# An mLSTM cell followed by a Fourier mixing block and an MLP: four shape-changing products and five steps moved within the order of issue

## The chip, the cores and the metric

The kernel runs on one core of a Trainium2 chip. A core has engines that run side by side, each with its own queue of instructions: TensorE (PE, matrix products; PEld are its weight loads), VectorE (DVE), ScalarE (ACT), GpSimd (POOL) and SyncE (SP, which here issues all the DMA transfers). An engine takes its instructions in the order in which the program issued them; semaphores make an engine wait for another one. PE writes its results into PSUM, eight banks of 2 KB per partition, from which DVE and ACT read them; everything else lies in SBUF. The metric is the device time of the whole program in microseconds (us), as the median of several runs.

## The reference, cut to what matters

Two blocks follow each other. The first is an mLSTM cell over 768 time steps, for 4 batches and 8 heads of width 40:

```python
for t in range(S):
    m_new = np.maximum(f_gate[:, :, t] + m, i_gate[:, :, t])
    f_stab = np.exp(f_gate[:, :, t] + m - m_new)
    i_stab = np.exp(i_gate[:, :, t] - m_new)
    m = m_new
    C = f_stab[:, :, None, None] * C + i_stab[:, :, None, None] * np.einsum('bhd,bhe->bhde', vt, kt)
    n = f_stab[:, :, None] * n + i_stab[:, :, None] * kt
    h_tilde = np.einsum('bhde,bhe->bhd', C, qt)
    nq = np.einsum('bhd,bhd->bh', n, qt)[:, :, None]
    denom = np.maximum(np.abs(nq), 1.0)
    y[:, :, t] = o * h_tilde / denom          # o is the sigmoid of o_gate
```

Its output, of width 8 x 40 = 320, goes into the second block:

```python
X = np.fft.fft(np.fft.fft(x, axis=1), axis=2)
u = x + np.real(X)
mu = np.mean(u, axis=-1, keepdims=True)
var = np.mean((u - mu) ** 2, axis=-1, keepdims=True)
un = (u - mu) / np.sqrt(var + 1e-06)
out = u + np.maximum(un @ w_ch1, 0.0) @ w_ch2     # w_ch1: 320 x 1280, w_ch2: 1280 x 320
```

All arithmetic is in fp32. PE makes two passes for each fp32 product, so the trace shows two MATMUL records for one product of the program (one for a transpose).

## The kernel before, in words

**The mLSTM** is worked in chunks of 128 time steps, six per batch. For a chunk c of batch b, PE makes the scores k x q (`mlstm_scores`, L465: 40 rows of weights, that is half of PE's rows, two heads side by side in the two halves), what the carried state contributes (`mlstm_from_state`, L479: full 128 x 128 products of the decayed queries `qg` with the state `C`, none for the first chunk), what the chunk itself contributes (`mlstm_from_chunk`, L486: 41 columns, half of PE's columns, onto the same PSUM tile `ph`) and the next state's increment (`mlstm_to_state`, L496, tile `pc`). Around them ACT makes the exponentials (L421), POOL the causal mask (L443), the decayed queries (L431), the weighted values (L437) and the decayed state (L455), and DVE multiplies scores by weights (`mlstm_weigh`, L471) and adds `pc` to the state (`mlstm_gather`, L515; in the same step ACT copies `ph` out, L517 or L524). Later the chunk is transposed on PE (`mlstm_turn`, L535, tile `px`) and finished on DVE (`mlstm_finish`, L544 to L550, five instructions that read `px`, the last writing the chunk's rows of `x`).

`ph`, `pc` and (but for the first four chunks of batch 0) `px` take turns in two PSUM buffers, in the order in which the program asks for them. A new tile waits until the readers of the tile before the last have left its buffer.

**The mixing block** replaces the two FFTs by products with tables of cosines and sines, folded by symmetry. `mix_fold` (L606 to L624, DVE and a few small POOL instructions) adds and subtracts pairs of chunks, (2,3), (1,4) and (0,5) in this order, through one buffer `eo` into `fe`. For batches 2 and 3 `mix_fold_again` (L626 to L645, with L638 on DVE and L639 to L642 on POOL) folds once more. Then come `mix_seq` and `mix_tail` (L686 to L698, tiles `pz`, `pzt`), `mix_feat` (L729), `mix_add` (L749 to L757), which also makes mean and variance, and the centring and the transposes (L765, L772, L777) into `uT`. `mix_rstd` (L785 to L795) makes 1/sqrt(var + 1e-6) by a bit trick and three Newton steps: four small instructions on DVE and twelve on POOL. It is read by `residual` (L966) only, after the MLP.

**The MLP** of batch 0 is plain (`mlp_in`, L837 and L841, ReLU on ACT L850; `mlp_out`, L960). Batches 1 to 3 use Strassen-Winograd sums: `mlp_block` has four steps per pair of hidden blocks, five pairs, with full products (L897) and, in step 2, eight passes with 64 rows of weights (L902, half of PE's rows). DVE adds partial results (L906: one in step 1, three after step 2's L902). The next pair's first product goes into the bank that the first of those three has just read, and L902 of the next step 2 goes on adding in a bank that step 1's L906 reads first. The output (`mlp_out_pair`, L1016) uses sums of the hidden blocks (L1002) and of the second weights (`out_weight_sums`, L988, four of them); `mlp_sums` (L885) and `weight_sums` (L875) prepare the same for the first layer.

**The order of issue** is written out by hand. `at(slot, phase, fn, *args)` files a step under a slot and a phase, and `run` issues all steps by (slot, phase):

```python
EVAC, FILL, MAIN, FILL_PE = range(4)
```

So in a slot come first the evacuations, then the filling work, then the MLP's own products (phase `MAIN`), then the filling products of PE (`FILL_PE`). Each engine's queue is this order, cut down to that engine. Batch b's chunk c begins at slot s = s0 + 3c with s0 = 0, 32, 50, 82; its scores come in slot s, its L479, L486 and L496 in slot s + 3, its gather in s + 4. The MLP of batch b begins at slot 31, 63, 95, 127; for batch 0 a half-row L841 stands in every second slot from 32 to 50, for the others L902 stands in every fourth slot from 65, 97 and 129. In slots 38, 44 and 50 (batch 1), 65 (batch 2) and 97 (batch 3) the order on PE is therefore: the MLP's products, ending with half-row ones, then L479, then (for the next chunk) L465, then L486 and L496.

Of the kernel before, what the change touches and what calls it, by code (L numbers as in the profile page):

```python
# [20 lines left out]
NT = S // L  # L21
# [5 lines left out]
NFF = DFF // L  # L27
TAIL = DM - 2 * L
TG = NT // 2
# [21 lines left out]
def kernel(  # L51
# [70 lines left out]
    def at(slot, phase, fn, *args):  # L122
        plan.setdefault((slot, phase), []).append((fn, args))
# [7 lines left out]
    EVAC, FILL, MAIN, FILL_PE = range(4)  # L131
# [405 lines left out]
    def mlstm_finish(b, c):  # L537

        k = chunks.pop((b, c))
        if c == 0:  # L540
# [9 lines left out]
        nc.vector.tensor_tensor(out=xs[b][:, c, 0:DM].rearrange("p (h d) -> p h d", d=D), in0=h1[:, :, 0:D], in1=sc,  # L550
                                op=OP.mult)

    def plan_mlstm(b, s0, stride=3):
        for c in range(NT):
            s = s0 + stride * c
            if b > 0:
                t = 22 + 2 * c if b == 1 and c < 3 else s - 5
                at(t, FILL, mlstm_load, b, c)
                at(t, FILL, mlstm_load_max, b, c)
                at(t, FILL, mlstm_load_decay, b, c)  # L560
                at(s, FILL, mlstm_load_o, b, c)
            if (b, c) > (0, 0):
                at(s, FILL, mlstm_exp, b, c, 0)
                at(s + 1, FILL - 0.5, mlstm_exp, b, c, NP)
                last = (b, c) == (0, NT - 1)
                at(s - 1 if last else s, FILL_PE + (2.05 if last else 2), mlstm_scores, b, c)
                if b > 0:
                    at(s + 1, FILL, mlstm_mask, b, c)
            at(s, FILL, mlstm_scale_v, b, c)
            at(s if (b, c) == (0, 2) else s + 1, FILL + 0.1, mlstm_scale_q, b, c)  # L570
            at(s + 2, FILL, mlstm_decay, b, c)
            end = (b, c) == (0, NT - 1)
            at(s + 1 if end else s + 2, FILL - 0.4 if end else FILL, mlstm_weigh, b, c)
            at(s + 2 if end else s + 3, FILL_PE, mlstm_from_state, b, c)
            at(s + 2 if end else s + 3, FILL_PE + (2 if end else 3), mlstm_from_chunk, b, c)
            at(s + 3, FILL_PE + 3, mlstm_to_state, b, c)
            at(s + 3 if end else s + 4, FILL, mlstm_gather, b, c)
            if b == 0:
                t, x = ((8, 11), (11, 14), (13, 14), (14, 15.5), (17, 18), (18, 21))[c]
            else:  # L580
                t = s + (8, 8, 7, 5, 5, 5)[c]
                x = t + 1
            at(t, FILL_PE + ((2.5 if c < 4 else 1) if b == 0 else 1), mlstm_turn, b, c, b == 0 and c < 4)
            at(x, FILL + 0.05, mlstm_finish, b, c)
# [212 lines left out]
    def plan_mix(b, s0, x_done, s_feat, s_add, s_turn):  # L797
        for j in range(TG):
            p = TG - 1 - j
            at(x_done[j], FILL + 0.5 if b < 2 else FILL_PE + 0.2, mix_fold, b, p)  # L800
            if b == 0:
                at((s0 - 4, s0 - 2, s0)[j], FILL_PE + 4, mix_seq, b, p, (0, 1))
                at((s0 - 2, s0 - 2, s0)[j], FILL_PE + 4, mix_tail, b, p)
            elif b == 1 or j == 0:
                if b > 1:
                    for step, slot in enumerate((x_done[0], x_done[-1] + 2, x_done[-1] + 6)):
                        at(slot, FILL_PE + 0.25, mix_fold_again, b, step)
                at(s0, FILL_PE + 4, mix_seq, b, p, (0,))
                at(s0 + 1, FILL_PE + 4, mix_seq, b, p, (1,))
                at(s0 + 2, FILL_PE + 4, mix_tail, b, p)  # L810
        for i in range(2):
            at(s0 + 1 if b == 0 else s0 + 1 + i, FILL, mix_seq_out, b, i)
        at(s0 + (1 if b == 0 else 3), FILL + 0.1, mix_tail_out, b)
        for p in range(TG):
            at(s_feat[p], FILL_PE + 4, mix_feat, b, p)
        for c, a, t in zip(ORDER, s_add, s_turn):
            at(a, FILL if b < 2 else MAIN + 0.5, mix_add, b, c)
            at(t, FILL + 0.1, mix_center, b, c)
            at(t, FILL_PE + (5 if b == 0 or c in ORDER[:4] else -0.1), mix_turn, b, c)
            if b > 0:  # L820
                at(t, FILL_PE + 6, mix_turn_out, b, c)
            elif t < s_mlp:
                at(t + 1, FILL + 0.2, mix_turn_out, b, c)
            else:
                at(t + 1, EVAC, mix_turn_out, b, c)
# [221 lines left out]
    def plan_mlp(b, s):  # L1047
        groups = range(NT // TG)
        for i in range(NFF // 2) if b > 0 else ():
            for step in range(4):  # L1050
                at(s, MAIN, mlp_block, b, i, step)
                s += 1
            end = i == NFF // 2 - 1
            for n, (gr, f) in enumerate(((1, 2 * i + 1), (1, 2 * i), (0, 2 * i))):
                at(*((s - 1, MAIN + (-0.1 if gr else 0.1)) if end else (s + n, MAIN + 0.5)), mlp_relu_in_place, gr, f)
        for gr in groups if b == 0 else ():
            for f in range(NFF):
                at(s, MAIN, mlp_in, b, gr, f)
                s += 1
                if f % 2:  # L1060
                    at(s, EVAC, mlp_relu, b, gr, f - 1)
                    at(s, EVAC, mlp_relu, b, gr, f)
        if b > 0:
            for j in range(1, 5):
                at(s - (5, 4, 3, 3)[j - 1], FILL_PE + 0.3, hidden_sums, 0, (j,), 0, NFF // 2 - 2)
            at(s, EVAC, hidden_sums, 0, (1, 2), NFF // 2 - 2, NFF // 2)
            at(s, MAIN + 0.1, hidden_sums, 0, (3, 4), NFF // 2 - 2, NFF // 2)
        for n in range(TG) if b > 0 else ():
            for step in range(4):
                at(s, MAIN, mlp_out_pair, b, n, step)  # L1070
                if n < TG - 1 and step > 1:
                    for j in (2 * step - 3, 2 * step - 2):
                        at(s, MAIN + 0.6, hidden_sums, n + 1, (j,))
                s += 1
        for gr in groups if b == 0 else ():
            for i in range(TG):
                for half in range(2):
                    at(s, MAIN, mlp_out, b, gr, i, half)
                    s += 1
                at(s, EVAC, mlp_store, b, gr, i)  # L1080
# [5 lines left out]

    def plan_batch(b, s_mlstm, s_mix, s_mlp):
        plan_mlstm(b, s_mlstm)
        done = [s_mlstm + 3 * (j + NT // 2) + 7 for j in range(NT // 2)]
        assert s_mix >= done[-1] and s_mlp >= s_mix + 9  # L1090
        late = [s_mlp + 2 * c for c in range(TG)]
        if b == 0:
            feat = [s_mix + 1, s_mix + 1, s_mlp + 3]
            turn = [s_mix + 2, s_mix + 3, s_mix + 4]
            add = turn + [s_mlp, s_mlp + 4, s_mlp + 6]
            late = [s_mlp + 2, s_mlp + 5, s_mlp + 7]
        else:
            feat = [s_mix + c for c in ((3, 4, 6) if b == 1 else (3, 4, 7))]
            add = [s_mix + c for c in ((4, 4, 5, 6, 7, 7) if b == 1 else (4, 4, 5, 6, 8, 9))]
            turn = [s_mix + c for c in ((5, 6, 6) if b == 1 else (6, 7, 8))]  # L1100
            late = [s_mix + c for c in ((7, 8, 8) if b == 1 else (9, 10, 10))]
            at(s_mlp, EVAC + 0.5, mlp_sums)
        plan_mix(b, s_mix, done, feat, add, turn + late)
        at(s_mlp + NFF, FILL + 0.6, mix_rstd, b)
        plan_mlp(b, s_mlp)

    s_mlp = 31
    plan_batch(0, 0, 22, s_mlp)
    plan_batch(1, 32, 54, s_mlp + MLP_SLOTS)
    plan_batch(2, 50, 83, s_mlp + 2 * MLP_SLOTS)  # L1110
    plan_batch(3, 82, 115, s_mlp + 3 * MLP_SLOTS)
    for n in range(4):
        at(s_mlp + 2 * NFF + 1 + n, FILL + 0.4, weight_sums, n)
        at((56, 57, 58, 72)[n], FILL + 0.4, out_weight_sums, n)

    at(60, FILL + 0.4, lambda: nc.gpsimd.memset(ds_sb[0:1, 0, 0, :], 1.0))

# [131 lines left out]
```

## Time and profile before

| | |
|---|---|
| median of 8 runs | 421.96 us (420.38 to 422.52) |
| the profiled execution | 420.93 us, span of its instructions 419.2 us |
| PE, DVE, ACT, POOL busy | 406.8, 288.0, 188.8, 113.3 us |
| PE's largest wait by releaser | L897 for DVE's L906, 1.6 us in two places |
| granted PE clock | 1.000 |

The span runs from the first to the last instruction of the program; the time of an execution is a little longer. A row of a timeline gives start and length in us, the engine, the source line and the instruction, with "output tile <- input tiles", and in brackets the idle time of the engine before it and what most likely ended it. Equal instructions that follow each other are one row ("x8"). Since PE's products overlap, their lengths overlap too, and the distance from one start to the next says what an instruction cost. The name after "<-" in brackets is inferred: a wait for DVE may be put down to the instruction next to the one that released it.

### The profile page before, as it was taken

How to read it: one execution, taken by the hardware profiler on the slowest of the kernel's cores; microseconds unless marked ns; L12 is line 12 of the kernel's file. 1: busy time of each engine (PE TensorE's matmuls, PEld its weight loads, DVE VectorE, ACT ScalarE, POOL GpSimd, SP SyncE). 2: the span in 40 equal slices, each digit the busy share in tenths (PEclk: the TensorE clock that was granted, in tenths of full speed). 3: DMA queues.
4: the chain of work that ended last, by engine and by line, in shares of the span. 5: the costliest groups of instructions: out<-in, count | busy, mean ns of one | idle time of the engine just before them, and what ended most of it. 6: DMA issues, size and time to landing. Idle time of an engine off the chain costs nothing.

```text
span 419.2 us, 8013 instructions
## 1 busy us (share of the span) xinstructions
PE 406.8 (97%) x2966; PEld 303.8 (72%) x2966; DVE 288.0 (69%) x682; ACT 188.8 (45%) x493; POOL 113.3 (27%) x194
## 2 busy tenths in 40 slices
PE   8999999999999999999899999999999999999997
PEld 6877455566567778777559998977559988555996
DVE  8788895777995638795965578795854686335652
ACT  6986375586561232654355413654442013355000
POOL 5564201468331520342131440342220000020000
PEclk9999999999999999999999999999999999999999
DMA  7879397557665154176200454210000000000010
GB/s 237 273 217 345 120 260 240 192 180 224 223 179 156 59 155 140 63 210 187 59 0 2 141 154 132 101 48 2 0 2 0 33 31 24 10 2 0 16 48 31
DMA packets 20549, 47.14 MB, mean 112 GB/s; under 512 B 2784, under 2 KB 9312, under 8 KB 20384
## 3 DMA queue, kind: packets, MB, share of 16 engines
q1 hardware_dynamic: 20512, 46.65, 35.8%
q8 instruction: 23, 0.38, 0.4%
q14 instruction: 14, 0.11, 0.1%
HBM read 42.52 MB, written 4.11 MB: 111 GB/s over the span
## 4 chain that ended last, share of the span: by engine, by line
PE 70%; DVE 13%; DMA 7%; issue 4%; POOL 3%; ACT 2%; SPq 1%; POOLq 0%; ACTq 0%; DVEq 0%
PE po L1016 19%; PE pm L897 15%; PE po L960 8%; PE pm L902 4%; PE ph L486 4%; PE ps L465 4%; PE ph L479 3%; PE pu L729 3%; DMA kvt<-in_kv 2%; PE put L772 2%; DMA qk<-in_qkT 2%; PE pz L698 2%; DMA raw<-in_w 2%; PE px L535 2%; PE pz L686 1%
## 5 line engine op out<-in xcount | busy, mean ns | idle before, releaser
L966 DVE SCALAR_TENSOR_TENSOR x<-po,rstd,x 128x160 f32<-128x160 f32 (+1 forms) x69 | 27.0, 394 | 41.7 <-PE po L1016 35.5
L906 DVE TENSOR_TENSOR h<-h,pm 128x384 f32<-128x384 f32 x60 | 30.5, 550 | 31.4 <-PE pm L897 16.1
L421 ACT ACTIVATE W<-W,colT 128x128 f32<-128x128 f32 x144 | 45.0, 396 | 0.0
L443 POOL TENSOR_SCALAR_AFFINE_SELECT W<-W 128x1024 f32<-128x1024 f32 x18 | 21.4, 1187 | 78.8 <-ACT W L421 58.4
L897 PE MATMUL pm<-uT,w_sb 128*128 128x384 f32 x90 | 37.5, 504 | 1.8 <-DVE h L906 1.6
L960 PE MATMUL po<-w_sb,h 128*128 128x320 f32 x120 | 34.4, 435 | 0.0
L471 DVE TENSOR_TENSOR W<-ps,W 128x512 f32<-128x512 f32 x48 | 30.7, 680 | 4.5 <-POOL W L443 4.3
L837 PE MATMUL pm<-uT,w_sb 128*128 128x384 f32 x80 | 29.9, 501 | 0.8 <-DVE x L749 0.5
L777 ACT COPY uT<-put 128x384 f32<-128x384 f32 x24 | 11.2, 478 | 40.2 <-PE put L772 40.2
L960 PEld LDWEIGHTS po<-w_sb,h 128*128 128x128 f32 x120 | 22.3, 190 | 9.4 <-issue 0.8
L1016 PE MATMUL po<-T,S 128*128 128x160 f32 x180 | 27.9, 302 | 0.3 <-DVE x L966 0.3
L465 PE MATMUL ps<-qk 40*128 40x128 f32 x384 | 27.8, 284 | 0.0
L792 POOL TENSOR_TENSOR t<-rstd 128x6 f32<-128x6 f32 x12 | 3.1, 258 | 88.5 <-DVE v L790 87.9
L1016 PEld LDWEIGHTS po<-T,S 128*128 128x128 f32 x180 | 25.5, 190 | 1.7 <-DVE x L966 0.5
L897 PEld LDWEIGHTS pm<-uT,w_sb 128*128 128x128 f32 x90 | 15.5, 190 | 15.4 <-DVE h L906 7.7
L1016 PE MATMUL po<-w_sb,h 128*128 128x160 f32 x180 | 26.5, 302 | 0.0
L465 PEld LDWEIGHTS ps<-qk 40*128 40x128 f32 x384 | 23.4, 188 | 4.1 <-issue 0.7
L1016 PEld LDWEIGHTS po<-w_sb,h 128*128 128x128 f32 x180 | 25.2, 190 | 1.3 <-DVE x L966 0.3
L486 PE MATMUL ph<-W,kvt 128*41 128x128 f32 x384 | 25.8, 277 | 0.0
L431 POOL TENSOR_TENSOR qg<-qk,Gb 128x512 f32<-128x512 f32 x18 | 25.4, 1414 | 0.4 <-DMA Gb<-G_d 0.3
L524 ACT COPY h<-ph 41x512 f32<-41x512 f32 (+1 forms) x16 | 9.3, 582 | 35.6 <-PE ph L486 35.4
L479 PEld LDWEIGHTS ph<-qg,C 128*128 128x128 f32 x160 | 19.9, 192 | 6.4 <-issue 2.5
(207 smaller groups left out, 864.1 us busy)
## 6 DMA issues: line engine op xcount, KB each, us to landing
W<-M_d SPq DMA_DIRECT2D x18, 512.0 KB
kvt<-in_kv SPq DMA_DIRECT2D x24, 324.0 KB
qk<-in_qkT SPq DMA_DIRECT2D x48, 160.0 KB
raw<-in_w SPq DMA_DIRECT2D x10, 640.0 KB
Gb<-G_d SPq DMA_DIRECT2D x36, 128.0 KB
so<-in_o SPq DMA_DIRECT2D x24, 160.0 KB
out<-x SPq DMA_DIRECT2D x24, 160.0 KB
ds_sb<-in_dft_s SPq DMA_DIRECT2D x1, 1155.0 KB
```

The source lines that it names most:

```text
L421: nc.scalar.activation(out=k.W[:, h, :], in_=M, func=AF.Exp, scale=-1.0, bias=colT[:, c, 0, b * H + h:b * H + h + 1])
L431: nc.gpsimd.tensor_tensor(out=k.qg, in0=k.qk[:, 0], in1=k.Gb, op=OP.mult)
L465: nc.tensor.matmul(k.ps[hip][:, p, :], k.qk[r, 1, p, :], k.qk[r, 0, p, :], start=True, stop=True)
L471: nc.vector.tensor_tensor(out=Wv, in0=k.ps[hip], in1=Wv, op=OP.mult)
L479: nc.tensor.matmul(k.ph[:, p, :], k.C[:, p, :], k.qg[:, p, :], start=(p == 0), stop=False, skip_group_check=True)
L486: nc.tensor.matmul(k.ph[hip * 64:hip * 64 + D1, p, :], k.v1[:, 2 * p + hip, :], k.W[:, 2 * p + hip, :], start=(c == 0 and p == 0), stop=Tr ...
L837: nc.tensor.matmul(k.pm[i], w1_sb[:, ch, f0:f0 + L], u[2 * ch], start=(ch == 0), stop=False)
L897: nc.tensor.matmul(bank, w, u, start=start, stop=True, skip_group_check=True)
L906: nc.vector.tensor_tensor(out=h, in0=h, in1=bank, op=OP.add)
L960: nc.tensor.matmul(k.po, hidden(gr, f)[:, i * L:(i + 1) * L], w2_sb[:, f, :], start=(f == 0), stop=(f == NFF - 1))
L966: nc.vector.scalar_tensor_tensor(out=u, in0=po, scalar=k.rstd[:, c:c + 1], in1=u, op0=OP.mult, op1=OP.add)
L1016: nc.tensor.matmul(po, a[:, f], w[:, f], start=start and f == 0, stop=f == half - 1, skip_group_check=True)
```

## The change

Six edits in the plan, none in the work itself. L479 of a chunk goes just ahead of the MLP's products of its slot where the slot is one of five listed (for four of the five there is such a step: chunk 1 and chunk 5 of batch 1, chunk 4 of batches 2 and 3), so that the half-row L465 follows the MLP's half-row products. The transposes of batch 1's chunk 3, and with them its finish, go from slot 46/47 to slot 48/49, and the fold of batch 1's chunks (2,3) from slot 48 to 49. The fold of chunks (0,5) of batches 2 and 3 goes one slot later (72 to 73, 104 to 105), behind that slot's MLP products instead of the slot's before. `mix_rstd` of batches 1 to 3 goes two slots later (73, 105, 137 to 75, 107, 139). The fourth sum of the second weights goes from slot 72 to 75.

```diff
+    slots_of_halves = (32, 38, 50, 65, 97)
+
     def plan_mlstm(b, s0, stride=3):
...
-            at(s + 2 if end else s + 3, FILL_PE, mlstm_from_state, b, c)
+            at(s + 2 if end else s + 3, MAIN - 0.1 if s + 3 in slots_of_halves else FILL_PE, mlstm_from_state, b, c)
             at(s + 2 if end else s + 3, FILL_PE + (2 if end else 3), mlstm_from_chunk, b, c)
...
-                t = s + (8, 8, 7, 5, 5, 5)[c]
+                t = s + (8, 8, 7, 7 if b == 1 else 5, 5, 5)[c]
                 x = t + 1
...
-            at(x_done[j], FILL + 0.5 if b < 2 else FILL_PE + 0.2, mix_fold, b, p)
+            at(x_done[j] + (b > 1 and j == TG - 1), FILL + 0.5 if b < 2 else FILL_PE + 0.2, mix_fold, b, p)
...
-        done = [s_mlstm + 3 * (j + NT // 2) + 7 for j in range(NT // 2)]
+        done = [s_mlstm + 3 * (j + NT // 2) + 7 + (b == 1 and j == 0) for j in range(NT // 2)]
...
-        at(s_mlp + NFF, FILL + 0.6, mix_rstd, b)
+        at(s_mlp + NFF + (2 if b > 0 else 0), FILL + 0.6, mix_rstd, b)
...
-        at((56, 57, 58, 72)[n], FILL + 0.4, out_weight_sums, n)
+        at((56, 57, 58, 75)[n], FILL + 0.4, out_weight_sums, n)
```

In the listing above and in the profile of before, lines have the numbers of the kernel before; the new kernel's are four higher from L553 on.

## The prediction

> **What bounds the kernel now.** I read the page first (busy shares, the chain that ended last), then the waits, then the timelines of TensorE and VectorE around every instruction that the diff moves.
>
> ```profile
> span 419.2 us, 8013 instructions
> ...
> PE 406.8 (97%) x2966; PEld 303.8 (72%) x2966; DVE 288.0 (69%) x682; ACT 188.8 (45%) x493; POOL 113.3 (27%) x194
> ...
> PE 70%; DVE 13%; DMA 7%; issue 4%; POOL 3%; ACT 2%; SPq 1%; POOLq 0%; ACTq 0%; DVEq 0%
> ```
>
> TensorE (PE) is busy for 97% of the span. From 110 us on the chain runs over PE with two short detours through VectorE (DVE), near 199 to 207 us and 294 to 301 us. So an edit pays only if it shortens PE's own row or one of the few waits left in it. PE's timeline, cut to the rows that matter (start, length, instruction, in brackets the idle time before it):
>
> ```profile
> 60.19 0.92 PE L841 MATMUL pm<-uT,w1t_sb 64*128 64x384 f32 x4
> 60.94 1.06 PE L465 MATMUL ps<-qk 40*128 40x128 f32 x16
> ...
> 109.85 1.13 PE L479 MATMUL ph<-qg,C 128*128 128x128 f32 x8 [0.64 <-DVE den L544]
> ...
> 183.90 0.60 PE L535 MATMUL px<-ident,h 128*128 128x128 f32 x4
> ...
> 185.72 1.56 PE L902 MATMUL pm<-uT,w1t_sb 64*128 64x384 f32 x8
> 187.22 1.16 PE L479 MATMUL ph<-qg,C 128*128 128x128 f32 x8
> 188.30 1.16 PE L465 MATMUL ps<-qk 40*128 40x128 f32 x16
> ...
> 197.95 1.56 PE L902 MATMUL pm<-uT,w1t_sb 64*128 64x384 f32 x8
> 199.51 0.91 PE L897 MATMUL pm<-uT,w_sb 128*128 128x384 f32 x2
> ...
> 204.66 1.85 PE L902 MATMUL pm<-uT,w1t_sb 64*128 64x384 f32 x8
> 207.56 0.91 PE L897 MATMUL pm<-uT,w_sb 128*128 128x384 f32 x2 [1.05 <-DVE h L906]
> ...
> 278.34 0.60 PE L535 MATMUL px<-ident,h 128*128 128x128 f32 x4
> ...
> 280.16 1.97 PE L902 MATMUL pm<-uT,w1t_sb 64*128 64x384 f32 x8
> ...
> 301.61 0.91 PE L897 MATMUL pm<-uT,w_sb 128*128 128x384 f32 x2 [0.54 <-DVE h L906]
> ```
>
> See three things. L479 is slower between half-row products than elsewhere. L902 to L897 takes 1.56 us at 197.95 but 2.90 at 204.66. At 109.85 PE waits for a chunk's finish. The DVE rows behind it:
>
> ```profile
> 184.24 0.49 DVE L550 TENSOR_TENSOR x<-px,so 128x320 f32<-128x320 f32 x1
> ...
> 203.45 0.98 DVE L988 TENSOR_TENSOR w_sb<-w_sb 128x800 f32<-128x800 f32 x1
> ...
> 206.96 1.48 DVE L906 TENSOR_TENSOR h<-h,pm 128x384 f32<-128x384 f32 x3
> ...
> 279.57 0.49 DVE L550 TENSOR_TENSOR x<-px,so 128x320 f32<-128x320 f32 x1
> ```
>
> **The change, part by part.** Nothing is added or taken away; the orders of ScalarE (ACT) and SP, all DMAs included, stay as they are.
>
> *Half-row products together.* Slot 32 of the five has no such step; in 38, 50, 65 and 97 (L479 now at 80.00, 119.07, 187.22, 282.06) L479 goes ahead of the MLP's products, and L465 follows the half-row products directly. Starts in slot 65 now: L902 185.72, L479 187.22, L465 188.30, L486 189.40, so 1.50 + 1.08 + 1.10 = 3.68 us. Without a change of shape at its edges L479 is eight passes of 0.111 = 0.89. L465 behind half-row products takes 0.99 (60.94 to 61.93). Half-row products ahead of L465 are 0.10 shorter (L841 60.19 to 60.94 is 0.75; ahead of L479, at 118.22, 0.85), so L902 takes 1.40. Sum 3.28: 0.40 less per slot, 1.60 in four.
>
> *What L479 now waits for.* It writes one of two PSUM buffers, which the transposed chunk of two turns earlier must have left. That is L550, the last instruction of a finish; at 109.85 L479 began 0.14 after such an L550 ended (109.71). Everything on PE stands behind a waiting L479.
> - Slot 65: PE is ready for it when L535 is over, 184.34. L550 ends 184.73, plus 0.14: 0.53 of wait. Net +0.13.
> - Slot 97: ready at 278.77; L550 ends 280.06, so 280.19 at best: 1.42. In exchange L902 no longer waits for DVE's L906 (280.16 to 282.06 is 1.90 instead of 1.50): -0.40. Net -0.40 - 0.40 + 1.42 = +0.62.
> - Slot 38: no finish in its way, and its inputs are ready (L431 ends 77.22, PE at 78.35): -0.40. This is ahead of 107 us, where DVE, POOL and ACT are nearly full; they follow through the transposes at 83.49, ACT L777, L850, L421, POOL L443 (86.55) and DVE L471. If a load held that chain, the gain would be 0.
> - Slot 50: see next.
>
> *Chunk 3's transposes from slot 46 to 48 (batch 1).* They were what made L479 at 109.85 wait: the two buffers came round to chunk 2, whose L550 ended at 109.71. L837 at 107.12 would have let it start at 109.06, and it then took 1.06 instead of 0.99: 0.79 + 0.07 = 0.86 saved. Now L479 takes a buffer that L515 left at 105.62. Late next: L479 of slot 50, now behind chunk 3's own finish. PE gets there at 119.07 - 0.40 (slot 38) - 0.86 (the transposes only change places), less the 1.59 that L837 and L841 took ahead of it (117.48 to 119.07): 116.2. DVE: chunk 2's finish over at 109.3, then L358, L360, L364, which took 3.94 at 111.26 and 2.33 at 91.21. L358 took 1.35 there beside POOL's L443 and takes 0.79 alone, and now starts before L443: 3.39, so L515 begins at 112.6; 0.65 for L515, 1.29 for L471, 1.71 for the finish, 0.14: 116.4. Wait 0.2, net -0.20; the wait lies between 0 (2.33 us) and 0.75 (3.94 us), and I take the value of 3.39, the row of the same three instructions with its one known difference.
> The Trainium skill, SBUF — State Buffer, section Who interferes with whom, has a harder rule: an instruction of VectorE with two SBUF inputs and a GpSimd read lock each other out, and the one that issues first keeps the port. L360 took 0.82 alone and 1.89 when POOL's L431 was already running, which agrees. By that rule L360 would now be first, keep its 0.82, and the wait could be 0; the sum would be 0.2 better than by the rows.
>
> *Fold, rstd and weight sum off the busy stretch (batch 2, slots 72 to 75).* L988 stood ahead of L906 (204.35), the fold (204.82, 1.59 to the next start) and rstd (206.41, 0.55) ahead of the three L906 at 206.96. They cost PE 207.56 - 204.66 - 1.55 = 1.35. In the new order L906 comes first, then fold 1.59, L638 0.47 (0.55 less the 0.08 by which neighbours overlap), L988 0.90, rstd 0.55: 3.51. The three L906 end 2.35 after L902 starts (198.90 + 1.40 against 197.95); L906 of the next block then ends at 2.35 + 3.51 + 0.55 = 6.41, and L902 comes 6.27 after its predecessor (212.28 - 204.66 - 1.35). 0.15 late: net -1.20, between -1.35 and -0.75 (0.6 late, as if the fold's 1.38 us L618 of 121.48 recurred for some of its length).
> Batch 3: the same without L988. 301.61 - 299.50 - 1.55 = 0.56; the work ends 0.76 ahead of the next L902: -0.56. Batch 1's fold and batch 3's rstd move where PE waits for neither.
>
> *Moved later, at no cost:* rstd's twelve POOL instructions (207.06 to 210.72) end near 214.7, after L639 to L642, which go first; the first reader, L966 of slot 83, comes near 223. L988's weights are read in slot 84. Were that cover gone, L966 and then PE would stand still by the difference.
>
> Sum: -0.40 (slot 38) - 0.86 (47) - 0.20 (50) + 0.13 (65) + 0.62 (97) - 1.20 - 0.56 = -2.47. Best ends: -4.8, with no wait in 65 and 97; worst ends: 0 - 0.4 + 0.3 + 0.4 + 0.9 - 0.75 - 0.4, about zero. The profiled execution took 420.93 (span 419.2 and 1.7 around it): 418.5. It lies 1.03 below the median of the eight, 421.96, so the forecast for a median is 419.5.
>
> **Rivals.**
> 1. The lead won before 125 us (1.46) is lost again: a load, or slot 50's finish at its bad end, holds PE. For: DMA is at 6 to 7 tenths there, and PE stands between three nearly full engines. Against: after 124 us DVE idles over 2 us twice for PE (127.94, 133.48), so it isn't ahead of PE. Left: -1.20 - 0.56 + 0.75 = -1.0, 420.9.
> 2. The DVE wait only moves one block on: the four postponed groups now all lie between two L906. For: 6.41 against 6.27 leaves no room. Against: no large POOL work beside them. At 1.2 us late the sum is -1.4: 420.5; with rival 1 too, no change.
> 3. Slower: the advanced L479 stand at the head of PE's queue behind finishes in slots 50, 65 and 97. The other gains are 0.40 + 0.86 + 1.20 + 0.56, and the shapes there give 1.20 and L902 0.40: the three waits must pass 4.6 us together, against 2.1 by the rows, for the time to rise; at 6 us it is 423.4. For: finishes follow four other DVE groups. Against: two of the three waits are read off PE-driven rows.
> 4. The shape change costs nothing where L465 follows L902: the rows at 60.94 are of L841, the same shape, so this is hardly open; 1.6 dearer, 421.1.
>
> **How the numbers follow.** The sum as it stands (-1.7 to -3.4) 0.58; rivals 1, 2 and 4 singly (-0.85 to -1.7) 0.22; two of them together, within 0.2% (0.84 us, about what a measurement of this kernel tells from no change) 0.12; rival 3 0.08. Faster 0.80, same 0.12, slower 0.08. Range: from -3.7 (waits of 65 and 97 half as long) to -0.8: 418.2 to 421.2, with about one in ten left out above and less below.
>
> **What would show it.** L479 near 108.3 without a wait; L902 to L465 without the 0.2 us steps; L479 waiting for a DVE finish by about 0.5 us in slot 65 and 1.4 in slot 97, as new rows of the waits; L902 to L897 back at 1.55 in batches 2 and 3, and the next L902 at most 1.7 us long. Wrong if PE waits over 0.5 us near 116, if the L906 wait reappears near 210, or if PE's lead at 120 us is gone at 165 us.

## The result and the profile after

The changed kernel takes 419.93 us (median of 14 runs, 418.75 to 421.27), the kernel before, timed beside it, 421.98 us (median of 38). The ratio is 0.9954 with a 95% interval from 0.9943 to 0.9964, so 1.5 to 2.4 us are won. The profiled execution of the changed kernel took 418.23 us. The page of the kernel after, the lines that answer to those shown of before:

```profile
span 416.5 us, 8020 instructions
...
PE 404.7 (97%) x2966; PEld 303.9 (73%) x2966; DVE 287.3 (69%) x682; ACT 188.9 (45%) x493; POOL 115.6 (28%) x194
...
PE 82%; DVE 8%; issue 3%; POOL 3%; ACT 2%; DMA 2%; POOLq 0%; ACTq 0%
```

PE is 2.1 us less busy with the same 2966 records of products. Its share of the chain rises from 70% to 82%, but this share says little by itself: in the eight kernels below it lies between 65% and 80%, and it doesn't follow their times. PE's timeline of the kernel after, at the places that the change touches:

```profile
77.92 1.05 PE L479 MATMUL ph<-qg,C 128*128 128x128 f32 x8
78.81 0.81 PE L841 MATMUL pm<-uT,w_sb 128*128 128x384 f32 x2
79.55 0.92 PE L845 MATMUL pm<-uT,w1t_sb 64*128 64x384 f32 x4
80.30 1.06 PE L465 MATMUL ps<-qk 40*128 40x128 f32 x16
81.29 1.08 PE L486 MATMUL ph<-W,kvt 128*41 128x128 f32 x16
...
107.79 1.05 PE L479 MATMUL ph<-qg,C 128*128 128x128 f32 x8
...
115.30 0.60 PE L535 MATMUL px<-ident,h 128*128 128x128 f32 x4
115.73 1.06 PE L479 MATMUL ph<-qg,C 128*128 128x128 f32 x8
...
181.77 0.60 PE L535 MATMUL px<-ident,h 128*128 128x128 f32 x4
182.74 1.13 PE L479 MATMUL ph<-qg,C 128*128 128x128 f32 x8 [0.38 <-DVE x L550]
...
202.74 1.56 PE L906 MATMUL pm<-uT,w1t_sb 64*128 64x384 f32 x8
204.30 0.91 PE L901 MATMUL pm<-uT,w_sb 128*128 128x384 f32 x2
...
209.01 2.07 PE L906 MATMUL pm<-uT,w1t_sb 64*128 64x384 f32 x8
211.01 0.91 PE L901 MATMUL pm<-uT,w_sb 128*128 128x384 f32 x2
...
277.37 1.13 PE L479 MATMUL ph<-qg,C 128*128 128x128 f32 x8 [1.26 <-DVE x L550]
...
297.37 1.56 PE L906 MATMUL pm<-uT,w1t_sb 64*128 64x384 f32 x8
298.92 0.91 PE L901 MATMUL pm<-uT,w_sb 128*128 128x384 f32 x2
```

Read it against the timeline of before. Half-row products (L845, was L841) and half-row L465 now follow each other directly: from each start to the next, L479 takes 0.89 us here, L845 0.75 and L465 0.99. L479 at 107.79 has no idle time before it (0.64 before), L479 at 115.73 none either. Two new waits stand ahead of L479 at 182.74 and 277.37. L906 to L901 (were L902 and L897) takes 1.56 us where it took 2.90, but the next pair, at 209.01, takes 2.00 where it took 1.55. VectorE's rows of the kernel after, behind these waits:

```profile
109.48 0.82 DVE L360 SCALAR_TENSOR_TENSOR m<-raw,m 128x640 f32<-128x640 uint32 x1
110.34 1.59 DVE L364 TENSOR_TENSOR w_sb<-m,e 128x640 f32<-128x640 f32 x1
...
182.11 0.49 DVE L550 TENSOR_TENSOR x<-px,so 128x320 f32<-128x320 f32 x1
...
206.44 0.32 DVE L617 TENSOR_TENSOR fe<-eo 128x159 f32<-128x159 f32 x1
206.87 0.56 DVE L642 TENSOR_TENSOR eo<-fe 128x384 f32<-128x384 f32 x1
207.34 0.99 DVE L992 TENSOR_TENSOR w_sb<-w_sb 128x800 f32<-128x800 f32 x1
208.25 0.28 DVE L789 TENSOR_SCALAR v<-x 128x6 f32<-128x6 f32 x1
...
208.93 0.55 DVE L910 TENSOR_TENSOR h<-h,pm 128x384 f32<-128x384 f32 x1
...
276.73 0.49 DVE L550 TENSOR_TENSOR x<-px,so 128x320 f32<-128x320 f32 x1
```

L479 begins 0.14 to 0.15 us after these two L550 end (182.60 and 277.22): the finish sets its start. L910 (was L906) at 208.93 ends at 209.48, after its block's products have begun.

**Shifts.** To put a number on each step I took the start of the same product in two profiles and followed the difference along the span: what the difference gains over a stretch is what that stretch won or lost. The first eleven rows add up to the difference of the two spans, to 0.03 us. All columns are against the profiled execution of before; a minus is time won. The eight on the right are the experiments, which are told below.

| step, us | predicted | after | e1 | e2 | e3 | e4 | e5 | e6 | e7 | e8 |
|---|---|---|---|---|---|---|---|---|---|---|
| start, to 60 us | | -0.07 | +1.10 | -0.01 | +1.09 | +1.06 | +0.44 | +0.07 | +0.48 | +0.26 |
| product at 70.05, which waits | | -0.43 | +0.38 | +0.61 | +0.10 | +0.48 | +0.05 | +1.24 | +0.09 | +1.03 |
| slot 38 | -0.40 | -0.39 | -0.40 | 0 | 0 | -0.39 | -0.39 | -0.39 | -0.39 | -0.39 |
| slots 39 to 45 | | +0.02 | +0.26 | +0.26 | +0.53 | +0.09 | +0.15 | +0.51 | +0.50 | +1.25 |
| slot 47 | -0.86 | -0.87 | +0.26 | -0.88 | +0.51 | -0.88 | -0.87 | -0.88 | -0.88 | -0.88 |
| slot 50 | -0.20 | -0.40 | -0.40 | 0 | 0 | -0.29 | -0.15 | -0.39 | +0.02 | -0.39 |
| slot 65 | +0.13 | +0.21 | +0.23 | 0 | 0 | 0 | -0.04 | +0.23 | -0.05 | +0.22 |
| batch 2, slot 73's block | -1.35 | -1.35 | 0 | 0 | -1.35 | -1.34 | -1.35 | -1.35 | -1.35 | -1.35 |
| batch 2, the block after | +0.15 | +0.45 | 0 | 0 | +0.44 | +0.44 | +0.45 | 0 | 0 | +0.44 |
| slot 97 | +0.62 | +0.69 | +0.69 | 0 | 0 | 0 | -0.46 | +0.70 | -0.45 | +0.70 |
| batch 3 | -0.56 | -0.55 | 0 | 0 | -0.55 | -0.55 | -0.55 | -0.55 | -0.55 | -0.55 |
| the change's own steps | -2.47 | -2.21 | +0.12 | -0.88 | -1.46 | -3.01 | -3.36 | -2.63 | -3.65 | -0.95 |
| measured, from the ratio | | -1.94 | +0.34 | -1.39 | -1.22 | -3.50 | -3.50 | -2.45 | -3.84 | -1.27 |

The sum of the own steps takes in the rows that a kernel's edits touch: slots 39 to 45 only for e8, which changes slot 44, and slot 47 neither for e1 nor for e3. The last row is the ratio less one, times the median of before beside the run; its intervals are 0.4 to 0.7 us to each side and stand with each run. Each kernel's sum of its own steps lies inside its interval. The first two rows and that of slots 39 to 45 differ between executions whatever the edit. They are read at the end.

### The profile page after: what moved, and what is told of

Same layout as the page of the kernel before. It is cut to its first block, busy times and chain, and to the rows that moved or that the text cites. A ratio compares the mean times of both kernels' runs of the same rounds, so it can differ in the third digit from the quotient of the medians.

```text
span 416.5 us, 8020 instructions
## 1 busy us (share of the span) xinstructions
PE 404.7 (97%) x2966; PEld 303.9 (73%) x2966; DVE 287.3 (69%) x682; ACT 188.9 (45%) x493; POOL 115.6 (28%) x194
## 4 chain that ended last, share of the span: by engine, by line
PE 82%; DVE 8%; issue 3%; POOL 3%; ACT 2%; DMA 2%; POOLq 0%; ACTq 0%
PE po L1020 19%; PE pm L901 16%; PE po L964 8%; PE pm L906 5%; PE ps L465 5%; PE ph L486 4%; PE pm L841 4%; PE pu L733 4%; PE ph L479 3%; PE px L535 2%; PE put L776 2%; PE pz L702 2%; DMA kvt<-in_kv 2%; PE pz L690 1%; PE pM L218 1%
## 5 line engine op out<-in xcount | busy, mean ns | idle before, releaser
L910 DVE TENSOR_TENSOR h<-h,pm 128x384 f32<-128x384 f32 x60 | 30.6, 550 | 32.5 <-PE pm L906 19.4
L443 POOL TENSOR_SCALAR_AFFINE_SELECT W<-W 128x1024 f32<-128x1024 f32 x18 | 21.5, 1195 | 81.0 <-ACT W L421 56.7
L901 PE MATMUL pm<-uT,w_sb 128*128 128x384 f32 x90 | 37.5, 504 | 0.2 <-DVE uT L889 0.2
L471 DVE TENSOR_TENSOR W<-ps,W 128x512 f32<-128x512 f32 x48 | 30.7, 680 | 4.5 <-POOL W L443 4.3
L841 PE MATMUL pm<-uT,w_sb 128*128 128x384 f32 x80 | 29.8, 499 | 0.7 <-DVE x L753 0.5
L465 PE MATMUL ps<-qk 40*128 40x128 f32 x384 | 27.4, 282 | 0.0
L465 PEld LDWEIGHTS ps<-qk 40*128 40x128 f32 x384 | 23.8, 188 | 4.7 <-issue 0.7
L431 POOL TENSOR_TENSOR qg<-qk,Gb 128x512 f32<-128x512 f32 x18 | 25.6, 1423 | 0.2
L901 PEld LDWEIGHTS pm<-uT,w_sb 128*128 128x128 f32 x90 | 15.5, 190 | 13.7 <-DVE h L910 6.0
L479 PEld LDWEIGHTS ph<-qg,C 128*128 128x128 f32 x160 | 20.1, 192 | 5.6 <-issue 2.1
L957 ACT ACTIVATE h<-h 128x384 f32<-128x384 f32 x45 | 23.1, 521 | 2.0 <-DVE h L910 2.0
```

What stands on the lines that cost most here:

```text
L431: nc.gpsimd.tensor_tensor(out=k.qg, in0=k.qk[:, 0], in1=k.Gb, op=OP.mult)
L465: nc.tensor.matmul(k.ps[hip][:, p, :], k.qk[r, 1, p, :], k.qk[r, 0, p, :], start=True, stop=True)
L471: nc.vector.tensor_tensor(out=Wv, in0=k.ps[hip], in1=Wv, op=OP.mult)
L479: nc.tensor.matmul(k.ph[:, p, :], k.C[:, p, :], k.qg[:, p, :], start=(p == 0), stop=False, skip_group_check=True)
L841: nc.tensor.matmul(k.pm[i], w1_sb[:, ch, f0:f0 + L], u[2 * ch], start=(ch == 0), stop=False)
L901: nc.tensor.matmul(bank, w, u, start=start, stop=True, skip_group_check=True)
```

## The experiments

**e1: only the four moves of L479.** The changed kernel with the other edits undone:

```diff
-                t = s + (8, 8, 7, 7 if b == 1 else 5, 5, 5)[c]
+                t = s + (8, 8, 7, 5, 5, 5)[c]
...
-            at(x_done[j] + (b > 1 and j == TG - 1), FILL + 0.5 if b < 2 else FILL_PE + 0.2, mix_fold, b, p)
+            at(x_done[j], FILL + 0.5 if b < 2 else FILL_PE + 0.2, mix_fold, b, p)
...
-        done = [s_mlstm + 3 * (j + NT // 2) + 7 + (b == 1 and j == 0) for j in range(NT // 2)]
+        done = [s_mlstm + 3 * (j + NT // 2) + 7 for j in range(NT // 2)]
...
-        at(s_mlp + NFF + (2 if b > 0 else 0), FILL + 0.6, mix_rstd, b)
+        at(s_mlp + NFF, FILL + 0.6, mix_rstd, b)
...
-        at((56, 57, 58, 75)[n], FILL + 0.4, out_weight_sums, n)
+        at((56, 57, 58, 72)[n], FILL + 0.4, out_weight_sums, n)
```

> Only the four moves of L479 ahead of the MLP's products (slots 38, 50, 65, 97) are made; chunk 3's transposes, the fold, rstd and the weight sum stand where they stood before. Sums against the kernel before. My theory (each step's term stands alone): -0.40 in slot 38, -0.40 to -0.20 in slot 50, +0.23 in slot 65, +0.65 in slot 97: between 0 and +0.3 us, ratio 1.000; L479 still waits about 0.8 us for chunk 2's finish in slot 47, and L479 has waits of about 0.5 us in slot 65 and 1.3 to 1.4 us in slot 97. Rival 'the lead before 125 us is absorbed': slots 38 and 50 give nothing, +0.9 us, ratio 1.002. Rival 'the change of shape costs nothing': no gain in any of the four slots, the two waits dearer, about +1.5 us, ratio 1.0035.

Measured: 422.71 us against 422.27, ratio 1.0008 (0.9994 to 1.0021), that is +0.34 us, between -0.25 and +0.89. PE's waits of e1 (total, times, longest):

```profile
PE ph L479 <- DVE x L550: 1.6, 2, 1.3
...
PE ph L479 <- DVE den L544: 0.9, 1, 0.9
...
PE pm L841 <- DMA qk<-in_qkT: 0.5, 1, 0.5
```

The four moves by themselves win nothing: what the two of batch 1 win (-0.40 each) is eaten by what the two of batches 2 and 3 lose, where the wait is longer than the gain of shape (+0.23, +0.69). The rival by which the change of shape costs nothing falls: slots 38 and 50 do win, and its +1.5 us is outside the interval. The rival that the early lead is absorbed (+0.9) is at the interval's edge, and the profile is in between: the wait of slot 47 that stays here is 0.9 us long and not 0.64. But e3, which moves nothing in slot 38, has 1.15 us there, so the longer wait is not proof that slot 38's gain was eaten.

**e2: only chunk 3's transposes, finish and fold of batch 1.** The changed kernel with the other edits undone:

```diff
-    slots_of_halves = (32, 38, 50, 65, 97)
+    slots_of_halves = ()
...
-            at(x_done[j] + (b > 1 and j == TG - 1), FILL + 0.5 if b < 2 else FILL_PE + 0.2, mix_fold, b, p)
+            at(x_done[j], FILL + 0.5 if b < 2 else FILL_PE + 0.2, mix_fold, b, p)
...
-        at(s_mlp + NFF + (2 if b > 0 else 0), FILL + 0.6, mix_rstd, b)
+        at(s_mlp + NFF, FILL + 0.6, mix_rstd, b)
...
-        at((56, 57, 58, 75)[n], FILL + 0.4, out_weight_sums, n)
+        at((56, 57, 58, 72)[n], FILL + 0.4, out_weight_sums, n)
```

> Only chunk 3's transposes, finish and fold of batch 1 are two, two and one slots later; everything else as before. My theory: the wait of L479 near 110 us goes, and the 0.8 us stay to the end: -0.8 us, ratio 0.998, with no wait over 0.2 us at L479 of slot 50, which stands behind the MLP's products here. Rival 'the lead before 125 us is absorbed': PE is 0.8 us ahead at 112 us and level again by 165 us, 0.0 us, ratio 1.000. Rival 'slot 50 now waits for chunk 3's finish': a new wait of 0.5 to 0.8 us at L479 near 118 us, -0.3 to 0.0 us.

Measured: 421.09 us against 422.27, ratio 0.9967 (0.9954 to 0.998): -1.39 us, between -1.94 and -0.84. The wait of slot 47 is gone for good, and the rivals (0.0, or -0.3 to 0.0 with a new wait in slot 50) fall. PE's and then VectorE's row of slot 47 in e2:

```profile
109.52 1.05 PE L479 MATMUL ph<-qg,C 128*128 128x128 f32 x8
```

```profile
107.41 0.49 DVE L344 TENSOR_SCALAR e<-raw 128x640 uint32<-128x640 uint32 x1 [1.98 <-DMA raw<-in_w]
...
110.69 0.49 DVE L550 TENSOR_TENSOR x<-px,so 128x320 f32<-128x320 f32 x1
```

VectorE stood 1.98 us for a load of weights here, and chunk 2's finish ended at 111.18; L479 began at 109.52 all the same. With the old order it would have had to wait until 111.18 + 0.14. In e1 and e3, where the old order stays, VectorE's L344 waits 0.35 and 0.73 us for this load, and L479 waits 0.90 and 1.15 us instead of 0.64. The row of e3:

```profile
112.09 1.13 PE L479 MATMUL ph<-qg,C 128*128 128x128 f32 x8 [1.15 <-DVE den L544]
```

So the wait that this step removes differs from one execution to the next, and the profile of before, where L344 had no wait for the load, shows the shortest of three (0.64, 0.90, 1.15). That would explain why the median gains more than the 0.88 read off against this one profile; since 0.88 lies inside the interval, it isn't shown.

**e3: only the fold, rstd and the weight sum.** The changed kernel with the other edits undone:

```diff
-    slots_of_halves = (32, 38, 50, 65, 97)
+    slots_of_halves = ()
...
-                t = s + (8, 8, 7, 7 if b == 1 else 5, 5, 5)[c]
+                t = s + (8, 8, 7, 5, 5, 5)[c]
...
-        done = [s_mlstm + 3 * (j + NT // 2) + 7 + (b == 1 and j == 0) for j in range(NT // 2)]
+        done = [s_mlstm + 3 * (j + NT // 2) + 7 for j in range(NT // 2)]
```

> Only the fold of the last pair in batches 2 and 3, rstd of batches 1 to 3 and the fourth weight sum are later; everything else as before. My theory: L902 to L897 at 204.7 us goes from 2.90 to 1.55 (-1.35), the next block of the MLP pays 0.45 of it back (L902 to L897 2.0 us there, VectorE being late with L906), and batch 3 gives -0.55: together -1.45 us, ratio 0.9965. Rival 'the wait of VectorE only moves one block on': the next block pays back all but 0.2, -0.5 us in all with batch 3, ratio 0.9988. Rival 'none of these waits bounds': 0.0 us.

Measured: 421.46 us against 422.27, ratio 0.9971 (0.9957 to 0.9985): -1.22 us, between -1.82 and -0.63. By its own steps -1.35 + 0.44 - 0.55 = -1.46. "Only moves one block on" (-0.5) is outside the interval, and the profile shows that a third of it does move on. Which of the groups moved away won how much, no run separates.

**e4: L479 back behind the MLP's products in slots 65 and 97.** Against the changed kernel:

```diff
-    slots_of_halves = (32, 38, 50, 65, 97)
+    slots_of_halves = (38, 50)
```

> The changed kernel, but L479 stays behind the MLP's products in slots 65 and 97 (the moves of slots 38 and 50 remain). My theory: the two moves undone here lose 0.23 and about 0.65 us, so this kernel is 0.9 us shorter than the changed one, about -2.9 us against the kernel before, ratio 0.993; the waits of L479 for L550 are gone from both slots, and PE waits about 0.4 us for VectorE's L906 in slot 97 again. Rival 'the head of the queue costs nothing, since what PE loses there it would have waited for later': no different from the changed kernel, -2.0 us, ratio 0.9954. Rival 'the shapes are worth more than the waits': 0.4 to 0.8 us longer than the changed one, ratio 0.997.

Measured: 419.12 us against 422.27, ratio 0.9917 (0.9901 to 0.9934): -3.50 us, between -4.18 and -2.79, where the changed kernel has -1.5 to -2.4. PE's timeline of e4 in slots 65 and 97:

```profile
183.97 0.60 PE L535 MATMUL px<-ident,h 128*128 128x128 f32 x4
184.40 0.81 PE L901 MATMUL pm<-uT,raw 128*128 128x384 f32 x2
```

```profile
279.30 1.97 PE L906 MATMUL pm<-uT,w1t_sb 64*128 64x384 f32 x8
281.20 1.16 PE L479 MATMUL ph<-qg,C 128*128 128x128 f32 x8
```

Behind L535 PE goes straight on with the MLP, and the late L906 of slot 97 (1.90 us to the next start) is back. These two moves are a loss, as forecast: leaving them out is faster than the change as a whole (the two intervals don't meet), by 0.90 us in the rows of slots 65 and 97.

**e5: the finish ahead of the weigh.** Against the changed kernel, for chunk 2 of batches 2 and 3:

```diff
-            at(x, FILL + 0.05, mlstm_finish, b, c)
+            at(x, FILL + (-0.05 if b > 1 and c == 2 else 0.05), mlstm_finish, b, c)
```

> The changed kernel, and in batches 2 and 3 chunk 2's finish (the one that ends with L550) goes on VectorE ahead of the weigh of its slot instead of behind it, so that the PSUM buffer of the advanced L479 comes free sooner in slots 65 and 97. My theory: the waits of L479 for L550 fall from 0.53 and 1.42 us to about 0.3 us each, 1.4 us less than the changed kernel: -3.4 to -3.7 us against the kernel before, ratio 0.992. Rival 'the wait passes to what now stands behind the finish' (the weigh, on which L515 and then PE depend): nothing won or up to 0.5 us lost against the changed kernel, ratio 0.9955 to 0.9965.

Measured: 418.70 us against 422.14, ratio 0.9917 (0.9901 to 0.9932): -3.50 us, between -4.18 and -2.87. VectorE's, then PE's timeline of e5:

```profile
276.69 0.49 DVE L550 TENSOR_TENSOR x<-px,so 128x320 f32<-128x320 f32 x1
277.10 1.28 DVE L471 TENSOR_TENSOR W<-ps,W 128x512 f32<-128x512 f32 x2
```

```profile
183.85 1.13 PE L479 MATMUL ph<-qg,C 128*128 128x128 f32 x8
...
277.33 1.13 PE L479 MATMUL ph<-qg,C 128*128 128x128 f32 x8
```

L479 of slot 97 still starts 0.15 us after L550's end (277.18). But PE is ready for it at 277.06 here and was at 275.95 in the kernel after, so measured from PE that end comes 1.15 us sooner, about the length of the weigh. A wait of 0.27 us is left in each of the two slots (some 0.3 was expected), and no new wait of PE for the weigh shows. The rows of slots 65 and 97 turn from +0.21 and +0.69 to -0.04 and -0.46. So it was the wait for the finish, and not the place of L479, that cost.

**e6: the weight sum later still.** Against the changed kernel:

```diff
-        at((56, 57, 58, 75)[n], FILL + 0.4, out_weight_sums, n)
+        at((56, 57, 58, 79)[n], FILL + 0.4, out_weight_sums, n)
```

> The changed kernel, with the fourth weight sum (L992 here, 0.99 us on VectorE) in slot 79 instead of 75, behind the MLP block in which PE still waited for VectorE's addition. My theory: the block after the cleared one goes from 2.0 us between the half-row products' second start and the next block back to 1.56, the 0.45 us that were given back are won: -2.4 us against the kernel before in this kernel's steps, ratio 0.9944 if the changed kernel is at 0.9954. Rival 'the fold alone makes VectorE late': nothing, ratio 0.9954. Rival 'the weight sum is now late for its reader in slot 84': a new wait on PE there, 0.3 to 1 us dearer, ratio 0.9965.

Measured: 419.60 us against 422.14, ratio 0.9942 (0.993 to 0.9955): -2.45 us, between -2.95 and -1.90. The gain over the changed kernel is smaller than these intervals; the profile has it. PE's timeline of e6:

```profile
205.04 1.56 PE L906 MATMUL pm<-uT,w1t_sb 64*128 64x384 f32 x8
206.60 0.91 PE L901 MATMUL pm<-uT,w_sb 128*128 128x384 f32 x2
...
211.31 1.56 PE L906 MATMUL pm<-uT,w1t_sb 64*128 64x384 f32 x8
212.87 0.91 PE L901 MATMUL pm<-uT,w_sb 128*128 128x384 f32 x2
```

In both blocks L906 to L901 now takes 1.56 us: without the weight sum's 0.91 us VectorE is in time, although the fold still stands there. Its reader in slot 84 shows no wait.

**e7: e5 and e6 together.**

```diff
-            at(x, FILL + 0.05, mlstm_finish, b, c)
+            at(x, FILL + (-0.05 if b > 1 and c == 2 else 0.05), mlstm_finish, b, c)
...
-        at((56, 57, 58, 75)[n], FILL + 0.4, out_weight_sums, n)
+        at((56, 57, 58, 79)[n], FILL + 0.4, out_weight_sums, n)
```

> The changed kernel with both of the edits above (the finish ahead of the weigh in batches 2 and 3, the weight sum in slot 79). My theory (steps in separate slots add up): 1.85 us less than the changed kernel, about -4 us against the kernel before, ratio 0.9905. Rival 'VectorE's delay only moves on again': no better than the finish alone, ratio 0.992. Rival 'both pass their waits on': as the changed kernel, ratio 0.9954.

Measured: 418.19 us against 422.14, ratio 0.9909 (0.9895 to 0.9922): -3.84 us, between -4.43 and -3.29. Its median is the lowest of all these kernels, though the intervals of e4 and e5 overlap its own, and by the ratios it lies 1.9 us below the changed one (forecast: 1.85). That the two edits add up is shown by the rows and not by the time: the rival by which e7 is no better than e5 (0.992) is just inside the interval, but the rows of slots 65 and 97 are e5's and the block after slot 73's has no debt, as in e6. The steps give -3.65; slot 50 gives nothing here, since L479 begins there 0.14 us after a finish, the wait that the prediction feared (its row counts 0.17 us of it as idle):

```profile
117.62 1.13 PE L479 MATMUL ph<-qg,C 128*128 128x128 f32 x8 [0.17 <-DVE x L550]
```

**e8: slot 44 too.** Against the changed kernel:

```diff
-    slots_of_halves = (32, 38, 50, 65, 97)
+    slots_of_halves = (38, 44, 50, 65, 97)
```

> The changed kernel with one more slot in the list, 44: there L479 is held by GpSimd's L431, whose result comes 0.05 us before L479 starts in the changed kernel's profile (98.15 and 98.20 us). My theory (an instruction put at the head of PE's queue makes everything behind it wait for its input): L479 can't start earlier, and the MLP's products that took 1.59 us ahead of it now come behind it; less the 0.40 us of the shapes, 0.9 to 1.2 us are lost there and kept, about -0.9 us against the kernel before, ratio 0.998. Rival 'the shapes are won wherever the step is put': 0.40 us better than the changed kernel, ratio 0.9944. Rival 'the loss is absorbed by a later wait of PE': PE is 1 us late at 102 us and level by 121 us, ratio 0.9954.

Measured: 421.05 us against 422.14, ratio 0.997 (0.9956 to 0.9983): -1.27 us, between -1.86 and -0.72. PE's timeline of e8:

```profile
99.92 1.16 PE L479 MATMUL ph<-qg,C 128*128 128x128 f32 x8 [1.49 <-POOL qg L431]
100.92 0.81 PE L841 MATMUL pm<-uT,w_sb 128*128 128x384 f32 x2
101.66 0.92 PE L845 MATMUL pm<-uT,w1t_sb 64*128 64x384 f32 x4
102.41 1.06 PE L465 MATMUL ps<-qk 40*128 40x128 f32 x16
```

PE stands still for 1.49 us ahead of L479, with the MLP's ready products behind it in the queue; 1.25 us are lost over slots 39 to 45, where the other kernels differ by 0.02 to 0.53 from before, and they stay lost to the end. "The shapes are won wherever the step is put" (-2.4 us) is outside the interval; "absorbed later" (-1.9) is too near the interval's end to fall by the timing, but the row of slot 47 is -0.88 as in the others and slots 48 to 65 give nothing back. This is the mechanism of the prediction's third rival (a product at the head of the queue holds all behind it), with GpSimd in the place of a finish, and here it does decide.

## Why the prediction was right

The direction, the likeliest case and the terms hold: 419.5 us were forecast and 419.93 measured, and five of the seven places came within 0.1 us, slot 50 and batch 2 inside their stated bounds. The misses partly cancel: slot 50 won 0.20 us more than forecast, batch 2 0.30 less, slots 65 and 97 lost 0.15 more.

- **Half-row products together.** -0.40 a slot: -0.39 or -0.40 in slot 38 in all seven kernels that do it, and the same in slot 50 wherever nothing is waited for. The three terms behind it, 0.89, 0.75 and 0.99, are the distances in slot 38 of the kernel after.
- **Chunk 3's transposes.** -0.86 was forecast, -0.87 or -0.88 came in all seven kernels that have the step. The size is read against an execution with a short wait (see e2).
- **Slot 50.** A wait of 0.2 was taken, between 0 and 0.75. In the six kernels that have both steps it is 0, 0.01, 0.01, 0.11, 0.25 and 0.42 us (0.40 less the row's gain). The step of 3.39 us for L358, L360 and L364 took 3.10 (108.75 to 111.85 in the kernel after): L360 took 0.82 and not 1.89, L364, now beside POOL's L443, 1.59 and not 0.82. So two terms were off in opposite directions, by 1.07 and 0.77 us, and that their sum came within 0.3 is luck. In before, e1 and e3 L360 began while POOL's L431 was running, took 1.89 us and ended 0.68 after it. In the seven kernels with chunk 3's step L360 is over before L431 begins; L443 begins during it, and L360 keeps its 0.82. There L364 begins while L443 is running, takes 1.59 to 1.69 and ends 0.68 after it (111.25 and 111.93 in the kernel after). Both agree with what the Trainium skill states (SBUF — State Buffer, section Who interferes with whom): between a VectorE instruction with two SBUF inputs and a GpSimd read, the one that issues first keeps the port. The prediction drew on this rule for L360 alone and not for L364. The rule's wait of 0 was nearer to the 0 of the kernel after than the rows' 0.2, but for the three instructions the rows' 3.39 were nearer to 3.10 than the 2.32 (3.39 less 1.07) that the rule for L360 alone would give. Where a wait came all the same, VectorE had less of a lead in slot 47 already: from the start of L471 (the two of slot 47) to that of L479 it is 1.29 us in e7, 1.54 in e5, 1.61 in e4, 1.71 in e6, 1.81 in the kernel after and 2.14 in e8; the waits are 0.42, 0.25, 0.11 and at most 0.01 in the last three.
- **Slots 65 and 97.** Waits of 0.53 and 1.42 us were worked out from L535's and L550's ends plus 0.14; the profile has 182.74 - 182.21 = 0.53 and 277.37 - 275.95 = 1.42, counted from when PE was ready, 0.44 after L535's start (the rows' 0.38 and 1.26 count from L535's printed end). Net +0.21 and +0.69 against +0.13 and +0.62: the products of L479 that follow a wait take 0.07 us more (1.13 instead of 1.06), which the sum left out. That these moves are a net loss, e4 shows.
- **Batch 2.** -1.35 exact; the debt in the next block was 0.45 instead of 0.15. This is the term that was mis-sized. The fold began 2.35 us after L906, as worked out. From there to the next addition 3.51 us of VectorE were counted, and it took 3.84 (205.09 to 208.93). The step from the fold to L638 (L642 after) was counted at 1.59 us, the distance to rstd, which in before followed the fold and overlapped it by 0.08; L642 reads what the fold has just written, begins 0.11 after its end, and the step takes 1.78. rstd's four instructions took 0.68 and not 0.55, the weight sum 0.91 and not 0.90. So VectorE is done 6.74 us after L906 instead of 6.41, where PE comes back after 6.27, and what was to be 0.15 late was 0.45. e6 shows that without the weight sum the debt is zero.
- **Batch 3.** -0.55 against -0.56.
- **The work moved later** costs nothing, as said: rstd's POOL instructions end at 214.31 in the kernel after (214.7 forecast), and their first reader comes at 221.44.
- **The rivals.** The early lead isn't lost in the kernel after: the shift is -2.14 at 121 us and -2.13 at 184. VectorE's delay moved one block on by a third. The third rival's waits were 2 us together and not 4.6.

In all, the steps give -2.21 in the profile, the forecast was -2.47, and the ratio gives -1.94 with an interval that holds the first and just misses the second.

## What to carry to other kernels

Moving a step to where its shape fits is only worth what is left after its inputs' and its buffer's release times are read there: at the head of an in-order queue a product makes everything behind it wait, ready or not. When a move uncovers such a wait, look at what stands ahead of the releaser on the other engine; putting the finish ahead of the weigh turned the two moves from a loss of 0.90 us into a gain of 0.50. When work is pushed to a later stretch, add it up there instruction by instruction against that stretch's period, with dependent neighbours counted at full distance.

## What the runs showed of the hardware

Executions of the same instructions differ mainly in three places before 102 us, and these differences, not the edits, move a single profile by up to 1.8 us (e6: 0.07 + 1.24 + 0.51). e2 and e3, whose edits all come later, show them: +0.61 at the second in e2, +1.09 at the first and +0.53 at the third in e3.

First, the eight small products of L218 at 4.6 us take 1.05 us in the profile of before and 1.92 in e1; e3 and e4 have 1.91. PE's timelines of before and of e1:

```profile
4.58 1.05 PE L218 MATMUL pM<-M,ident 128*128 128x128 f32 x8
```

```profile
4.75 1.92 PE L218 MATMUL pM<-M,ident 128*128 128x128 f32 x8
```

This is TensorE's clock. Eight of the ten traces hold a record of the span in which the full clock was granted. It begins at 4.33 us in before, 4.49 in after, 4.63 in e2, 4.81 in e5, 4.92 in e8, 5.38 in e7, 6.71 in e4 and 7.26 in e3. L218's products that start ahead of that time stand 0.21 us apart, those behind it 0.11, and in e7 the distance changes in the middle of the eight, at 5.38. e1 and e6 hold no record, and the granted clock of 1.00 that the profile's views print for these first microseconds is no reading: they print it where there is no record too. What sets the moment at which the full clock begins, no run here shows.

Second, the product at 70.05 us waits 0 to 1.4 us, put down to a load (before, e1, e8) or to ACT's L854 (e2 to e7).

Third, L465 of slot 45 took 1.74 us in e3, e6 and e7 and 1.16 in the other six that leave slot 44 alone. In these three its weight loads wait for VectorE's L471, 0.29 us at the longest, and VectorE's L344, some 3.5 us earlier, waited 2.26, 2.49 and 2.33 us for its load of weights, against 0.83 to 2.14 in the other six. Why the loads land at different times, no run here shows.

By the table none of it is caught up later. The profiled execution of before had nearly the short form of all three, and stands 1 us below its median; another kernel compared with it by one profile alone can look almost 2 us worse than it is. The shifts from one place to the next are free of that.
